# A reciprocal in place of the second decay scan, and four smaller moves, in a gated-linear-attention and router kernel

## The chip, the cores and the metric

The kernel runs on one core of a Trainium2 chip, in one launch. The metric is the device time of that core in microseconds; lower is better.

## What is computed

The first part is gated linear attention over 4 batches, 8 heads, 768 steps and a head size of 48. A state of 48x48 per head decays row by row with alpha and takes in one outer product per step. The second part sends each of the 3072 rows to one of 8 experts, by the largest cosine, and runs that expert's two layers (384 to 1024 to 384).

```python
def _attn_ref(q, k, v, alpha):
    state = np.zeros((B, H, D, D)); y = np.zeros_like(q)
    for t in range(S):
        state = alpha[:, :, t, :, None] * state + np.einsum('bhd,bhe->bhde', k[:, :, t], v[:, :, t])
        y[:, :, t] = np.einsum('bhd,bhde->bhe', q[:, :, t], state)
    return y
...
def _moe_ref(x, expert_emb, tau, w1, w2):
    xn = x / (np.linalg.norm(x, axis=-1, keepdims=True) + 1e-06)
    en = expert_emb / (np.linalg.norm(expert_emb, axis=-1, keepdims=True) + 1e-06)
    logits = xn @ en.T / tau
    expert_idx = np.argmax(logits, axis=1)
    probs = np.exp(logits - logits.max(-1, keepdims=True))
    probs /= probs.sum(-1, keepdims=True) + 1e-09
    gate_w = probs[np.arange(N), expert_idx]
    for e in range(E):
        mask = expert_idx == e
        h = np.maximum(x[mask] @ w1[e], 0.0)
        out[mask] = gate_w[mask, None] * (h @ w2[e])
    return out
```

## The kernel before

**The attention part** works on 24 chunks of 128 steps (6 per batch), all 8 heads at once. The tiles `at`, `kt`, `qt` and `vt` hold alpha, k, q and v of a chunk, with steps on the partitions; heads are padded from 48 to 64 columns. `load` (L410) issues the four transfers of a chunk on SP's queue and clears row 0 of the alpha tile on POOL, after the transfer. `turned` (L400) transposes a tile on PE into PSUM, two heads at a time, which gives four blocks of 128 steps along the free dimension.

`decays` (L420) makes the decay factors within a chunk. Let a(t) be alpha at step t of the chunk. The scan at L433 runs backward over the transposed alpha and leaves in `r` at step t the product of a(t+1) to the chunk's last step; since row 0 of the alpha tile is zero, one scan over all 512 columns restarts at each block. `kr` (L440) is k times `r`. The inverse of `r` is what q needs: a reciprocal of the first column of each block (L443, four elements) is put into the tile `ini`, and a forward scan (L447) multiplies alpha on from there, so that its result `a` is 1/`r` at every step. ACT copies the transposed q out of PSUM (`qc`, L454), and POOL multiplies it by `a` into `qs` (L455). `end` (L450) is the decay over the whole chunk; it takes alpha's first rows from `al0`, a small table of the first row of every chunk, transposed once.

A chunk then goes through a pipeline of several iterations of the main loop (L592): `keys_back` transposes `kr` back (L464) for the state's update, `scores` multiplies `kr` and `qs` (L515) and masks the result on DVE (`sm`, L519), `update` adds to the carried state (L492, L504), `mix_states` and `mix_chunk` make the output (L529, L541), `rows` turns it into rows with logits (L554, L560). `choose` and `place` pick the expert for groups of chunks with short DVE operations and find each token's row; `to_rows` scatters the rows to a buffer `xs` in DRAM through POOL's queue.

Two preparations come after the first chunk's work: `prepare` (L238) loads the expert embeddings, tau and alpha's first rows, normalises the embeddings (`embp`) and fills `sel` and `al0`; `routing_constants` (L111) makes masks and index tables.

**The expert part** starts with an early block of the expert that is first in turn (EARLY = 2 blocks of 128 tokens), whose first layer is already run among the last chunks. `gates` (L684) computes gate weights and output rows: the early block writes them to `gt_s[1]` and `sx_s[1]`, which expert 1 uses as well (L843). `to_rows(pads...)` fills the ends of the experts' blocks in `xs` with blank rows, eight transfers in a row on POOL's queue (L645); `fetch` reads an expert's rows back on SP's queue; `second_layer` ends in `scatter` (L665), an indirect transfer on POOL's queue that reads its row numbers from the `sx` tile.

The order of the work on each engine comes from a scheduler that knows the dependencies and the order of the program text; on each engine, and on each DMA queue, the instructions then run strictly in that order.

Of the kernel before, what the change touches and what calls it, by code (L numbers as in the profile page):

```python
# [27 lines left out]
def kernel(  # L28
# [155 lines left out]
    with ExitStack() as c1:  # L184
# [13 lines left out]
        NR = 3  # L198
        r_s = [keep.tile([P, NP * P], FP32, name=f"r{i}") for i in range(NR)]

        ini_s = [keep.tile([P, NP * P], FP32, name=f"ini{i}") for i in range(2)]
        inr = keep.tile([P, NP * P], FP32, name="inr")

        ND = 3
# [2 lines left out]
        def fixed_parts():  # L207
            for i in range(NBUF):
                nc.gpsimd.memset(at_s[i][:, :, D:DP], 1.0)
                nc.vector.memset(kt_s[i][:, :, D:DP], 0.0)  # L210
                nc.vector.memset(qt_s[i][:, :, D:DP], 0.0)
                if i == 0:
                    nc.gpsimd.memset(inr, 0.0)
                    for p in range(NP - 1):
                        nc.gpsimd.memset(inr[:, p * P + P - 1 : (p + 1) * P], 1.0)
                    for j in range(NR):
                        nc.vector.memset(r_s[j][:, NP * P - 1 :], 1.0)
                if i < 2:
                    nc.vector.memset(ini_s[i], 0.0)
            make_upper_triangular(nc, causal[:, 0], val=1.0, diag=True)  # L220
            for i in range(NBV):
                nc.vector.memset(vt_s[i][:, :, D:DP], 0.0)
            for i in range(ND):
                nc.gpsimd.memset(dec_s[i], 0.0)
# [10 lines left out]

        al0 = keep.tile([P, NP, NS], FP32, name="al0")

        def prepare():  # L238
            emb = work.tile([E, DM], FP32, name="emb", bufs=1)
            nc.scalar.dma_start(out=emb, in_=expert_emb)  # L240
            nc.scalar.dma_start(out=rtau, in_=tau.to_broadcast([P, 1]))
            a0 = work.tile([NS, H, DP], FP32, name="a0", bufs=1)
            nc.gpsimd.memset(a0[:, :, D:DP], 1.0)
            for b in range(B):
                nc.scalar.dma_start(
                    out=a0[b * NCH : (b + 1) * NCH, :, 0:D], in_=a_r[b, :, 0]
                )
            nc.vector.reciprocal(rtau, rtau)
            e2 = work.tile([E, DM], FP32, name="e2", bufs=1)
            en = work.tile([E, 1], FP32, name="en", bufs=1)  # L250
            nc.scalar.activation(e2, emb, AF.Square, accum_out=en)
            nc.scalar.activation(en, en, AF.Sqrt)
            nc.vector.tensor_scalar(en, en, 1e-6, None, ALU.add)
            nc.vector.reciprocal(en, en)
            nc.vector.tensor_tensor(en, en, rtau[:E], ALU.mult)
            embp = work.tile([E, H, DP], FP32, name="embp", bufs=1)
            nc.gpsimd.memset(embp, 0.0)
            nc.vector.tensor_scalar(
                embp[:, :, 0:D], emb.rearrange("e (h d) -> e h d", d=D), en, None, ALU.mult
            )  # L260
            pe = ps_tr.tile([P, NP, E], FP32, tag="tr", name="pe")
            for p in range(NP):
                nc.tensor.transpose(
                    pe[:, p], embp[:, 2 * p : 2 * p + 2].rearrange("e h d -> e (h d)"),
                    ident[:E, :E],
                )
            nc.gpsimd.memset(sel, 0.0)
            for p in range(NP):
                nc.gpsimd.tensor_copy(sel[0:DP, p, 0:D], ident[0:DP, 0:D])
                nc.gpsimd.tensor_copy(sel[DP:P, p, D : 2 * D], ident[DP:P, DP : DP + D])  # L270
            nc.vector.tensor_copy(sel[:, :, 2 * D :], pe)
            p0 = ps_tr.tile([P, NP, NS], FP32, tag="tr", name="p0")
            for p in range(NP):
                nc.tensor.transpose(
                    p0[:, p], a0[:, 2 * p : 2 * p + 2].rearrange("s h d -> s (h d)"),
                    ident[:NS, :NS],
                )
            nc.vector.tensor_copy(al0, p0)

        def to_rows(rows, x):  # L280
            ins = nc.gpsimd.indirect_dma_start(  # L281
# [118 lines left out]
        def turned(t, name):  # L400
# [6 lines left out]
                )  # L407
            return pt

        def load(s):  # L410
            b, c = divmod(s, NCH)
            i = s % NBUF
            nc.sync.dma_start(out=at_s[i][:, :, 0:D], in_=a_r[b, c])

            nc.gpsimd.memset(at_s[i][0:1], 0.0)
            nc.sync.dma_start(out=kt_s[i][:, :, 0:D], in_=k_r[b, c])
            nc.sync.dma_start(out=qt_s[i][:, :, 0:D], in_=q_r[b, c])
            nc.sync.dma_start(out=vt_s[s % NBV][:, :, 0:D], in_=v_r[b, c])

        def decays(s):  # L420

            c = s % NCH
            d = st[s]
            i = s % NBUF
            L = NP * P  # L430
            pa = turned(at_s[i], "pa")
            r = r_s[s % NR]
            nc.vector.tensor_tensor_scan(  # L433
                r[:, L - 2 :: -1], pa[:, L - 1 : 0 : -1], inr[:, L - 2 :: -1],
                1.0, ALU.mult, ALU.add,
            )
            pk = turned(kt_s[i], "pk")
            d["kr"] = kr = work.tile([P, NP, P], FP32, name="kr", bufs=3)
            krf = kr.rearrange("p n t -> p (n t)")
            nc.vector.tensor_tensor(krf, pk, r, ALU.mult)  # L440
            rv = r.rearrange("p (n t) -> p n t", t=P)
            ini = ini_s[s % 2]
            nc.vector.reciprocal(  # L443
                ini.rearrange("p (n t) -> p n t", t=P)[:, :, 0:1], rv[:, :, 0:1]
            )
            a = work.tile([P, L], FP32, name="a")
            nc.vector.tensor_tensor_scan(a, pa, ini, 0.0, ALU.mult, ALU.add)  # L447
            if c > 0:
                d["end"] = end = work.tile([P, NP, 1], FP32, name="end", bufs=3)
                nc.gpsimd.tensor_tensor(end, rv[:, :, 0:1], al0[:, :, s : s + 1], ALU.mult)  # L450
            pq = turned(qt_s[i], "pq")
            d["qs"] = qs = work.tile([P, NP, P], FP32, name="qs", bufs=4)
            qc = work.tile([P, NP * P], FP32, name="qc")
            nc.scalar.copy(qc, pq)  # L454
            nc.gpsimd.tensor_tensor(qs.rearrange("p n t -> p (n t)"), qc, a, ALU.mult)  # L455

        def keys_back(s):

# [129 lines left out]
        send = []  # L588
        fixed_parts()
        load(0)  # L590
        load(1)
        for s in range(NS + 4):  # L592
            if s + 2 < NS:
                load(s + 2)
            if 0 <= s - 1 < NS:
                keys_back(s - 1)
            if 0 <= s - 2 < NS:
                mix_states(s - 2)
            if 0 <= s - 3 < NS:
                rows(s - 3)  # L600
            if s < NS:
                decays(s)
            if 0 <= s - 1 < NS:
                decay_state(s - 1)
                scores(s - 1)
                update(s - 1)
            if 0 <= s - 2 < NS:
                mix_chunk(s - 2)
            if s == 0:
                prepare()  # L610
                routing_constants()
            if 4 <= s < 4 + NXG:
                nc.gpsimd.memset(xg_s[s - 4], 0.0)
            if s == 8:
                nc.gpsimd.memset(blank, 0.0)
            if s == NS:
                turn_early()
                first_layer_early(0, 2)
            if s == NS + 1:
                first_layer_early(2, 4)  # L620

            r = s - 4
            if r >= 0:
                g = group_of[r]
                if r == GROUPS[g][1] - 1:
                    place(g)
                    if r == S0 - 1:
                        first_expert()
            for c in send[:] if s >= S0 + 3 else send[:1]:
                to_rows(dest[:, c : c + 1], st[c]["x"])  # L630
                send.remove(c)
            if r == S0 - 1:
                fetch_early()
                for i in range(2):
                    weights(i)
            r = s - 3
            if 0 <= r < NS:
                g = group_of[r]
                if r == GROUPS[g][1] - 1:
                    choose(g)  # L640
            if s == NS + 2:
                first_layer_early(4, FT)
        counts()
        for i in range(E):
            to_rows(pads[:, i : i + 1], blank)  # L645
            if i < 2:
                fetch(i)


    with ExitStack() as c3:  # L650
# [189 lines left out]
                        half_block(w1_t, w2_t, xT, gate[0:HALF], col[0:HALF])  # L840


        egt, esx = gt_s[1], sx_s[1]  # L843
        gates(exg[:, 0:EARLY], egt[:, 0:EARLY], esx[:, 0:EARLY], EARLY)
        for t in range(EARLY):
            if t == EARLY - 1:
# [7 lines left out]
        for i in range(E):  # L854
            if i + 2 < E:
                weights(i + 2)
                fetch(i + 2)
            run(i)
            run_extra(i)
# [32 lines left out]
```

## Time and profile before

| | us |
|---|---|
| median of 3 runs | 487.36 (486.78 to 490.43) |
| profiled execution, its own time | 490.61 |
| its span, first to last instruction | 488.8 |
| PE busy | 450.3 (92%) |
| DVE busy | 195.1 (40%) |
| POOL busy | 146.8 (30%) |
| ACT busy | 135.3 (28%) |
| mean granted TensorE clock | 0.981 |

The profile is one execution. PE is the matmul engine, PEld its weight loads, DVE the vector engine, ACT the scalar engine, POOL the general engine, SP the engine that issues most of the transfers. A group line reads: source line, engine, operation, output<-inputs by the program's names, shape, count | busy time in us, mean of one in ns | idle time of the engine before them in us, and what ended it. Waits read: engine, tile and line that waited <- what it waited for: us in total, times, the longest. The timeline reads: start in us, length in us, engine, line, operation, count [idle before <- what ended it].

### The profile page before, as it was taken

The numbers are of one execution on the slowest core, as the hardware profiler recorded it, in microseconds if no ns is written. First come the engines' busy times: TensorE is split into PE (matmuls) and PEld (weight loads), VectorE is DVE, ScalarE is ACT, GpSimd is POOL, SyncE is SP. The second block draws the span as 40 slices with busy tenths as digits, with TensorE's granted clock in tenths as the row PEclk, the third lists the DMA queues.
The fourth block names the chain that finished last, engine by engine and source line by source line (L and its number), as shares of the span: only waits on it lengthen the run. The fifth ranks groups of instructions, "written<-read, shape, count | busy, mean of one in ns | idle before, by whom it ended". The sixth has DMA issues, their size and how long they took to land. (4 is left out here: it accounts for less than half of the span.)

```text
span 488.8 us, 8137 instructions
## 1 busy us (share of the span) xinstructions
PE 450.3 (92%) x2964; PEld 327.1 (67%) x2965; DVE 195.1 (40%) x505; ACT 135.3 (28%) x304; POOL 146.8 (30%) x256
## 2 busy tenths in 40 slices
PE   2699979979898999969999999999999999999993
PEld 1699968969787888657555655557556655555551
DVE  3889878887687952530131121110131121111000
ACT  3133323323232323461460240200560160110200
POOL 5855556656545642620101001000101101002001
PEclk9999999999898999988999999999999999999997
DMA  9999877776691297491900903600800710000000
GB/s 142 163 153 163 165 132 165 123 153 134 127 172 25 83 333 268 116 311 56 334 1 34 330 3 106 248 16 19 311 20 34 262 64 32 16 0 34 12 16 31
DMA packets 119189, 59.98 MB, mean 123 GB/s; under 512 B 102119, under 2 KB 113648, under 8 KB 119144
## 3 DMA queue, kind: packets, MB, share of 16 engines
q1 hardware_dynamic: 115040, 49.18, 43.1%
q0 software_dynamic: 3728, 10.16, 5.9%
q8 instruction: 27, 0.44, 0.4%
q14 instruction: 18, 0.15, 0.1%
q10 hardware_dynamic: 376, 0.05, 0.1%
HBM read 49.72 MB, written 11.45 MB: 125 GB/s over the span
## 5 line engine op out<-in xcount | busy, mean ns | idle before, releaser
L728 PE MATMUL ph<-xT,w 128*128 128x384 f32 (+1 forms) x384 | 119.6, 462 | 1.6 <-PEq L813 0.4
L739 PE MATMUL pyo<-w,hT 128*128 128x384 f32 x352 | 118.3, 497 | 0.0
L666 POOL DMA_INDIRECT out_dram<-y,sx x27 | 26.1, 966 | 248.4 <-DVE y L742 171.2
L739 PEld LDWEIGHTS pyo<-w,hT 128*128 128x128 f32 x352 | 67.7, 194 | 46.7 <-issue 2.6
L728 PEld LDWEIGHTS ph<-xT,w 128*128 128x128 f32 x384 | 67.6, 190 | 44.4 <-issue 5.2
L742 DVE TENSOR_SCALAR y<-pyo,gt 128x384 f32<-128x384 f32 x24 | 14.8, 617 | 121.1 <-PE pyo L739 121.1
L732 ACT ACTIVATE hT<-ph 128x384 f32<-128x384 f32 (+1 forms) x64 | 28.5, 459 | 115.6 <-PE ph L728 115.6
L515 PE MATMUL sc<-qs,kr 64*128 64x128 f32 x384 | 30.1, 298 | 12.3 <-POOL qs L455 12.3
L455 POOL TENSOR_TENSOR qs<-qc,a 128x512 f32<-128x512 f32 x24 | 30.5, 1272 | 25.6 <-DVE a L447 22.9
L515 PEld LDWEIGHTS sc<-qs,kr 64*128 64x128 f32 x384 | 25.2, 198 | 16.8 <-POOL qs L455 13.6
L519 DVE TENSOR_TENSOR sm<-sc,causal 128x512 f32<-128x512 f32 x48 | 30.5, 676 | 1.3 <-PE sc L515 1.3
L433 DVE TENSOR_TENSOR_SCAN r<-pa,inr 128x511 f32<-128x511 f32 x24 | 29.2, 1218 | 3.2 <-PE pa L403 2.8
L547 ACT COPY yT<-py 128x512 f32<-128x512 f32 x24 | 14.1, 586 | 58.8 <-PE py L541 58.8
L447 DVE TENSOR_TENSOR_SCAN a<-pa,ini 128x512 f32<-128x512 f32 x24 | 29.3, 1223 | 0.9
L281 POOL DMA_INDIRECT xs<-x,dest x24 | 24.0, 999 | 15.2 <-DVE dest L330 5.2
L541 PE MATMUL py<-sm,vt 128*64 128x128 f32 x384 | 26.5, 282 | 0.0
L682 DVE COPY xT<-pxg 128x384 f32<-128x384 f32 (+1 forms) x30 | 14.7, 498 | 28.9 <-PE pxg L681 28.8
L554 PE MATMUL px<-sel,yT 128*128 128x104 f32 x192 | 25.5, 276 | 0.0
L476 POOL TENSOR_TENSOR dec<-state,end 64x256 f32<-64x256 f32 x40 | 24.3, 608 | 2.7 <-DVE state L504 0.7
L554 PEld LDWEIGHTS px<-sel,yT 128*128 128x128 f32 x192 | 23.4, 192 | 0.8 <-ACT yT L547 0.5
L529 PE MATMUL py<-qs,dec 128*128 128x128 f32 x160 | 22.0, 281 | 0.5 <-DVE state L504 0.5
L541 PEld LDWEIGHTS py<-sm,vt 128*64 128x64 f32 x384 | 21.7, 143 | 0.6
(161 smaller groups left out, 522.5 us busy)
## 6 DMA issues: line engine op xcount, KB each, us to landing
w<-in_moe_w_dram SPq DMA_DIRECT2D x16, 1536.0 KB, 11.4
at<-in_alpha_dram SPq DMA_DIRECT2D x24, 192.0 KB, 5.4
kt<-in_k_dram SPq DMA_DIRECT2D x24, 192.0 KB, 4.0
qt<-in_q_dram SPq DMA_DIRECT2D x24, 192.0 KB, 5.5
vt<-in_v_dram SPq DMA_DIRECT2D x24, 192.0 KB, 3.6
xg<-xs SPq DMA_DIRECT2D x22, 196.5 KB, 6.7
xg<-xs SPq DMA_DIRECT2D x8, 98.2 KB, 5.7
out_dram<-y,sx POOLq DMA_INDIRECT x27, 2.6
```

The source lines that it names most:

```text
L433: nc.vector.tensor_tensor_scan(r[:, L - 2 :: -1], pa[:, L - 1 : 0 : -1], inr[:, L - 2 :: -1], 1.0, ALU.mult, ALU.add,)
L447: nc.vector.tensor_tensor_scan(a, pa, ini, 0.0, ALU.mult, ALU.add)
L455: nc.gpsimd.tensor_tensor(qs.rearrange("p n t -> p (n t)"), qc, a, ALU.mult)
L476: nc.gpsimd.tensor_tensor(dec[sl, :, hh], carried["state"][sl], d["end"][sl].to_broadcast([DP, NP, DP]), ALU.mult,)
L515: nc.tensor.matmul(sc[:, hh, p], lhsT=kr[sl, p], rhs=qs[sl, p], start=True, stop=True)
L519: nc.vector.tensor_tensor(sm[:, hh], sc[:, hh], causal.to_broadcast([P, NP, P]), ALU.mult)
L541: nc.tensor.matmul(py[DP * hh : DP * hh + DP, p], lhsT=vt[:, 2 * p + hh], rhs=sm[:, hh, p], start=("dec" not in d and p == 0), stop=True, ...
L554: nc.tensor.matmul(px[:, p], lhsT=yT[:, p], rhs=sel[:, p], start=True, stop=True)
L666: ins = nc.gpsimd.indirect_dma_start(out=out, out_offset=bass.IndirectOffsetOnAxis(ap=col, axis=0), in_=y, in_offset=None, bounds_check=N - 1,
L728: nc.tensor.matmul(ph, lhsT=w1_t[:, i, f * P : (f + 1) * P], rhs=xT[:, i], start=(i == 0), stop=(i == KT - 1),)
L732: nc.scalar.activation(hT[:, f], ph, AF.Relu)
L739: nc.tensor.matmul(py, lhsT=hT[:, f], rhs=w2_t[:, f], start=(f == 0), stop=(f == FT - 1),)
```

## The change

Six edits. (1) In `decays` the reciprocal is taken of the whole of `r` (128x512, on DVE) and multiplies q; the forward scan, the four-element reciprocal and the `ini` tiles go. (2) Row 0 of the alpha tiles is cleared once at the start; the loads write rows 1 to 127, as two transfers of 112 and 15 rows. (3) The transfer of `vt` of a chunk is issued with the next chunk's loads. (4) The preparations are split: the loads come first, `al0` follows chunk 0's decays, the logits' part chunk 1's, the routing constants chunk 2's; these and the clearing of `xg` and `blank` are queued behind the last DVE and POOL instructions of that chunk's `decays`. (5) Only two of the eight blank fillings stand ahead of the expert part in the text; the other six stand with the fetch of their expert. (6) The early block has gate and row tiles of its own, `egt` and `esx`.

```diff
-        ini_s = [keep.tile([P, NP * P], FP32, name=f"ini{i}") for i in range(2)]
...
         def fixed_parts():
             for i in range(NBUF):
                 nc.gpsimd.memset(at_s[i][:, :, D:DP], 1.0)
+
+                nc.gpsimd.memset(at_s[i][0:1], 0.0)
...
-                if i < 2:
-                    nc.vector.memset(ini_s[i], 0.0)
...
-        def prepare():
-            emb = work.tile([E, DM], FP32, name="emb", bufs=1)
-            nc.scalar.dma_start(out=emb, in_=expert_emb)
-            nc.scalar.dma_start(out=rtau, in_=tau.to_broadcast([P, 1]))
+        emb = work.tile([E, DM], FP32, name="emb", bufs=1)
+
+        def prepare_loads():
             a0 = work.tile([NS, H, DP], FP32, name="a0", bufs=1)
-            nc.gpsimd.memset(a0[:, :, D:DP], 1.0)
+            nc.vector.memset(a0[:, :, D:DP], 1.0)
             for b in range(B):
                 nc.scalar.dma_start(
                     out=a0[b * NCH : (b + 1) * NCH, :, 0:D], in_=a_r[b, :, 0]
                 )
+            nc.scalar.dma_start(out=emb, in_=expert_emb)
+            nc.scalar.dma_start(out=rtau, in_=tau.to_broadcast([P, 1]))
+            return a0
+
+        def prepare_first(a0):
+
+            p0 = ps_tr.tile([P, NP, NS], FP32, tag="tr", name="p0")
+            for p in range(NP):
+                nc.tensor.transpose(
+                    p0[:, p], a0[:, 2 * p : 2 * p + 2].rearrange("s h d -> s (h d)"),
+                    ident[:NS, :NS],
+                )
+            nc.vector.tensor_copy(al0, p0)
+
+        def prepare_logits():
+
             nc.vector.reciprocal(rtau, rtau)
...
+        AROW = P - 15
+
         def load(s):
...
+            if s < NS:
+                b, c = divmod(s, NCH)
+                i = s % NBUF
+                for p0, p1 in ((1, AROW), (AROW, P)):
+                    nc.sync.dma_start(out=at_s[i][p0:p1, :, 0:D], in_=a_r[b, c, p0:p1])
+                nc.sync.dma_start(out=kt_s[i][:, :, 0:D], in_=k_r[b, c])
+                nc.sync.dma_start(out=qt_s[i][:, :, 0:D], in_=q_r[b, c])
+            if s > 0:
+                b, c = divmod(s - 1, NCH)
+                nc.sync.dma_start(out=vt_s[(s - 1) % NBV][:, :, 0:D], in_=v_r[b, c])
+
+        def behind(s):
+
+            queue = ExitStack()
+            for call in st[s]["last"]:
+                queue.enter_context(tc.issue_after(call.ins))
+            return queue
 
         def decays(s):
...
             pk = turned(kt_s[i], "pk")
+            ri = work.tile([P, L], FP32, name="ri")
+            nc.vector.reciprocal(ri, r)
             d["kr"] = kr = work.tile([P, NP, P], FP32, name="kr", bufs=3)
             krf = kr.rearrange("p n t -> p (n t)")
-            nc.vector.tensor_tensor(krf, pk, r, ALU.mult)
-            rv = r.rearrange("p (n t) -> p n t", t=P)
-            ini = ini_s[s % 2]
-            nc.vector.reciprocal(
-                ini.rearrange("p (n t) -> p n t", t=P)[:, :, 0:1], rv[:, :, 0:1]
-            )
-            a = work.tile([P, L], FP32, name="a")
-            nc.vector.tensor_tensor_scan(a, pa, ini, 0.0, ALU.mult, ALU.add)
-            if c > 0:
-                d["end"] = end = work.tile([P, NP, 1], FP32, name="end", bufs=3)
-                nc.gpsimd.tensor_tensor(end, rv[:, :, 0:1], al0[:, :, s : s + 1], ALU.mult)
+            by_dve = nc.vector.tensor_tensor(krf, pk, r, ALU.mult)
...
-            nc.gpsimd.tensor_tensor(qs.rearrange("p n t -> p (n t)"), qc, a, ALU.mult)
+            by_pool = nc.gpsimd.tensor_tensor(
+                qs.rearrange("p n t -> p (n t)"), qc, ri, ALU.mult
+            )
+            if c > 0:
+                d["end"] = end = work.tile([P, NP, 1], FP32, name="end", bufs=3)
+                rv = r.rearrange("p (n t) -> p n t", t=P)
+                nc.gpsimd.tensor_tensor(end, rv[:, :, 0:1], al0[:, :, s : s + 1], ALU.mult)
+            d["last"] = by_dve, by_pool
...
         load(0)
+        a0 = prepare_loads()
         load(1)
         for s in range(NS + 4):
-            if s + 2 < NS:
+            if s + 2 <= NS:
                 load(s + 2)
...
+            if s == 0:
+                with behind(s):
+                    prepare_first(a0)
...
-            if s == 0:
-                prepare()
-                routing_constants()
+            if s == 1:
+                with behind(s):
+                    prepare_logits()
+            if s == 2:
+                with behind(s):
+                    routing_constants()
             if 4 <= s < 4 + NXG:
-                nc.gpsimd.memset(xg_s[s - 4], 0.0)
+                with behind(s):
+                    nc.gpsimd.memset(xg_s[s - 4], 0.0)
             if s == 8:
-                nc.gpsimd.memset(blank, 0.0)
+                with behind(s):
+                    nc.gpsimd.memset(blank, 0.0)
...
-        for i in range(E):
+        for i in range(2):
             to_rows(pads[:, i : i + 1], blank)
-            if i < 2:
-                fetch(i)
+            fetch(i)
...
-        egt, esx = gt_s[1], sx_s[1]
+        egt = xp.tile([P, EARLY], FP32, name="egt")
+        esx = xp.tile([P, EARLY], I32, name="esx")
...
             if i + 2 < E:
                 weights(i + 2)
+                to_rows(pads[:, i + 2 : i + 3], blank)
                 fetch(i + 2)
             run(i)
```

More of the change, by code (lines that the diff above doesn't have):

```diff
@@ L271, in prepare @@
             nc.vector.tensor_copy(sel[:, :, 2 * D :], pe)
[L272 to L276, printed above, removed]
-                )
-            nc.vector.tensor_copy(al0, p0)
         def to_rows(rows, x):
@@ L408, in turned @@
             return pt
+        AROW = P - 15
         def load(s):
[L411 to L418, printed above, removed]
+            if s < NS:
[13 more added lines that the diff above has]
+            return queue
         def decays(s):
@@ L437, in decays @@
             pk = turned(kt_s[i], "pk")
+            ri = work.tile([P, L], FP32, name="ri")
+            nc.vector.reciprocal(ri, r)
             d["kr"] = kr = work.tile([P, NP, P], FP32, name="kr", bufs=3)
             krf = kr.rearrange("p n t -> p (n t)")
-            nc.vector.tensor_tensor(krf, pk, r, ALU.mult)
-            rv = r.rearrange("p (n t) -> p n t", t=P)
-            ini = ini_s[s % 2]
-            nc.vector.reciprocal(
-                ini.rearrange("p (n t) -> p n t", t=P)[:, :, 0:1], rv[:, :, 0:1]
-            )
-            a = work.tile([P, L], FP32, name="a")
-            nc.vector.tensor_tensor_scan(a, pa, ini, 0.0, ALU.mult, ALU.add)
-            if c > 0:
-                d["end"] = end = work.tile([P, NP, 1], FP32, name="end", bufs=3)
-                nc.gpsimd.tensor_tensor(end, rv[:, :, 0:1], al0[:, :, s : s + 1], ALU.mult)
+            by_dve = nc.vector.tensor_tensor(krf, pk, r, ALU.mult)
             pq = turned(qt_s[i], "pq")
```

## The prediction

> **What bounds the kernel now.** I read the busy tenths first, to see which engine fills which stage.
>
> ```profile
> PE   2699979979898999969999999999999999999993
> DVE  3889878887687952530131121110131121111000
> ```
>
> A slice is 12.2 us. Up to slice 14 (about 170 us) the 24 attention chunks run, with PE and DVE both at 7 to 9 tenths; from there on PE is at 9 and DVE nearly idle. The expert stage belongs to PE, and nothing in the change shortens PE's work. So the attention stage decides, and in it the two busiest engines. The windows give their shares and a clock that I need later:
>
> ```profile
> 24.00:170.00 146.00, 134.18 (x1630) 122.93 (x1629) 122.17 (x248) 46.81 (x102) 85.28 (x151) 0.98 0.73 132
> 217.20:224.00 6.80, 6.09 (x12) 3.56 (x13) 2.34 (x10) 1.62 (x6) 0.00 (x0) 0.50 0.70 254
> ```
>
> Columns: window, length, busy PE, PEld, DVE, ACT, POOL, PE clock, DMA share, GB/s. From 24 to 170 us PE is busy 92%, DVE 84%, POOL 58%. The timeline has the first scan (L433) of chunk 2 at 24.5 and of chunk 23 at 170.0 us: 21 chunks in 145.5 us, 6.93 us each, of which DVE works 122.17 / 21 = 5.82. The best six chunks (24.5 to 60.9) take 6.07 each. PE sets the pace, with about 1.1 us of slack on DVE per chunk. The groups show the operations in question and the one stall of PE:
>
> ```profile
> L515 PE MATMUL sc<-qs,kr 64*128 64x128 f32 x384 | 30.1, 298 | 12.3 <-POOL qs L455 12.3
> L433 DVE TENSOR_TENSOR_SCAN r<-pa,inr 128x511 f32<-128x511 f32 x24 | 29.2, 1218 | 3.2 <-PE pa L403 2.8
> L447 DVE TENSOR_TENSOR_SCAN a<-pa,ini 128x512 f32<-128x512 f32 x24 | 29.3, 1223 | 0.9
> ```
>
> PE waits 12.3 us in all for qs, six times: where choose puts its small operations ahead on DVE.
>
> **The reciprocal.** Removed per chunk: the scan L447, 1.22 us, and the four-element reciprocal L443, whose ordinary duration is 0.17 (its mean of 0.22 holds one of 1.43). Added: a reciprocal of 128x512. No row shows one that large. The nearest are the small ones of the gates, beside another operation at the same place:
>
> ```profile
> L711 DVE RECIPROCAL gt<-gt 128x4 f32<-128x4 f32 x7 | 1.2, 178 | 0.2
> L710 DVE TENSOR_SCALAR gt<-gt 128x4 f32<-128x4 f32 x7 | 1.2, 169 | 0.2
> L710 DVE TENSOR_SCALAR gt<-gt 128x2 f32<-128x2 f32 x2 | 0.3, 168 | 0.1
> L711 DVE RECIPROCAL gt<-gt 128x2 f32<-128x2 f32 x2 | 0.3, 166 | 0.1
> ```
>
> Two more elements cost the reciprocal 12 ns and TENSOR_SCALAR 1 ns. A reduction goes from 170 ns (128x16, L709) to 183 (128x32), under 1 ns an element. So the reciprocal's slope is 6 ns an element: 178 + 508 x 6 = 3226 ns. The cheap end takes kr (L440, 128x512 in 718 ns) as one pass at the ordinary rate: 0.7 us. The dear end puts all that the four-element row has above a one-element operation on its elements: above L255 (147 ns) that is 31 / 4 = 7.8 ns and 4.1 us for 512, above L253 (142 ns) 9 ns and 4.7 us. I take 3.2, the difference between rows of the same operation at the same place; 0.7 and 4.1 to 4.7 stay for the range.
>
> The Trainium skill ("VectorE: DVE Perf Modes", section "Walkthrough: the 8-slice pipeline in each mode") says that Reciprocal runs on an iterative divide with a repeat count of 8, which speaks against this edit. Read as 8 cycles an element, at the 0.96 GHz that the skill gives VectorE ("Trainium Kernel Development and Optimization", section "NeuronCore Architecture"), that would be an estimated 4.3 us and a total near 532 us; the measured 12 ns for two elements fits it only in part.
>
> DVE per chunk becomes 5.82 - 1.22 - 0.17 + 3.23 = 7.66 us, more than PE's 6.07. The bound changes hands. An engine that bounds is still not busy all the time (DVE's best ten microseconds, 165 to 175, show 9.62), and pa of the next chunk stands on PE behind pkb, which waits for kr, and kr now stands behind the reciprocal. At 95% a chunk is 8.05 us: 21 x 8.05 = 169.1, against 145.5: **+23.6**.
>
> **The beginning.** The timeline from 4 to 12 us:
>
> ```profile
> 4.77 1.11 PE L403 MATMUL pa<-ident,at 128*128 128x128 f32 x4 [4.77 <-POOL at L415]
> 9.92 0.51 POOL L415 MEMSET at<- 1x512 f32 x1 [5.21 <-DMA at<-in_alpha_dram]
> 10.53 0.51 POOL L257 MEMSET embp<- 8x512 f32 x1
> 11.08 0.56 DVE L258 TENSOR_SCALAR embp<-emb,en 8x384 f32<-8x384 f32 x1 [2.80 <-POOL embp L257]
> 11.57 1.20 DVE L433 TENSOR_TENSOR_SCAN r<-pa,inr 128x511 f32<-128x511 f32 x1
> ```
>
> pa of chunk 0 is on PE at 4.8, its scan on DVE only at 11.6: DVE stands at embp, which waits for POOL, where the memset of row 0 waits for the second alpha load. The change takes both away (row 0 is cleared once, ahead of all loads; embp comes after chunk 1). The scan then starts at about 5.9. Chunk 1 follows after 1.22 + 3.23 + 0.70 and cold pkb and pa of 1.1 each, 7.3 us later (13.2), chunk 2 some 7.7 later (20.9, against 24.5): **-3.6**. What was moved now lies on the engine that bounds: the logits' six DVE operations (1.3 us) and the routing constants (L119 to L122, 3.4 us here, two of them stretched beyond 1 us beside a memset on POOL). I count **+2** of at most 4.7. The moved POOL work (sel, embp, three xg memsets of 1.40, blank 0.42) goes behind qs on POOL, which has 42% free; without that cover it is some 8 us.
>
> **The loads.** 24 memsets of 0.516 go, 12.4 us of POOL that cost nothing after the start. 24 more DMAs are issued on SP, at 0.37 to about 0.5 us; SP mostly waits for buffers, so only the first counts, and it is offset by the half microsecond of memset before pa. vt one chunk later and its buffer long free: nothing; the data of a chunk took SP some 4.9 us at the start, less than a chunk.
>
> **The end.** After the last scan the reciprocal ends 3.2 us later where the old pair, with kr, took 2.1: **+1.1**, partly covered by the early expert's matmuls. Then the own egt and esx. Around 215 us the waits are:
>
> ```profile
> DVE sx L700 <- DMA out_dram<-y,sx: 5.2, 1, 5.2
> PE pxg L681 <- DVE xT L682: 3.7, 1, 3.7
> ```
>
> sx of expert 1 may not be written until the early scatter has read its indices; the xT copies stand behind it on DVE, and PE stops for 3.7 us. Then comes the window at clock 0.50 above: the 16 matmuls pyo take 8.2 us there, where 26 took 8.63 at full clock (5.3 for 16), 2.9 more. With own tiles both go: at most 6.6, at least nothing if the rows of expert 1 are what is late next. I take **-5**. The skill's "TensorE: Matmul & The Clock Gate" (Part 1, the HAM clock gate) lets half rate follow an idle window of about 3.4 us, which fits this stop; by its rule the 2.9 goes with the stop. Six of eight pads still stand ahead of the first scatter; two fewer save 2.6 us of POOL, which PE does not wait for.
>
> **Sum.** 23.6 - 3.6 + 2 + 1.1 - 5 = +18.1 us. The profiled execution took 490.6 (span 488.8); the median of the runs is 487.4, so I put 18 on that: 505.
>
> **Rivals.** (1) The reciprocal is cheap, 0.7 us: DVE falls to 5.1 us a chunk, PE stays the bound, the stalls for qs shrink. 21 chunks at about 6.3 are 132 (-13), the beginning gains 7 (chunk 2's scan at about 16, since its alpha had landed by the memset at 15.7, less the moved small operations), the end 5: 462, 25 us faster. For it: reductions and TENSOR_TENSOR run at 1 ns an element, and 12 ns on so small an operation is near the scatter of those rows (one reciprocal of four took 166). Against it: 13 of 14 four-element ones lie at 177 or 178. The sign turns where the reciprocal takes about 2.4 us (a chunk of 7.2), 4.4 ns an element. (2) The dear end: at 4.1 us a chunk is busy 8.53 and takes 8.98, +43 for 21 chunks and +40 with the other terms (chunk 2's scan at 22.7, the tail at +2.0): 528; at 4.7 likewise 543; in the middle 535. (3) About 2.3 us and an even result, 488, if part of the 12 ns is a fixed cost. That the reciprocal were not executed or merged away is not possible: it is one instruction per chunk on DVE ahead of kr.
>
> **Chances.** Forecast (492 to 516, reciprocal 2.7 to 3.6 us) 0.55; dear 0.20; cheap 0.19; even 0.06. A measurement tells about 1% from no change here. Faster comes from the cheap case, slower from the first two and little of the third: 0.19, 0.05, 0.76. The range leaves out the cheap case and reaches to the dear end: 485 to 536; the forecast's own is 492 to 516.
>
> **What would show it.** The 128x512 reciprocal near 3.2 us; DVE above 93% from 20 to 190 us and PE nearer 75%, waiting for kr at pkb instead of for qs; first scan at 6 us, last near 190; no wait for the scatter before expert 1. It is wrong if the reciprocal's row shows under 2.4 us, or if PE's waits for kr grow so long that the clock column falls to 0.5 in the chunks.

## The result, and the profile after

| | before | after |
|---|---|---|
| median, us | 487.37 (486.78 to 490.43) | 514.18 (511.8 to 518.37) |
| profiled execution, span, us | 488.8 | 516.6 |
| mean granted TensorE clock | 0.981 | 0.952 |

The change makes the kernel slower: the ratio is 1.0546 (95% interval 1.046 to 1.0632). The busy tenths of the page, in 40 slices of 12.9 us:

```profile
PE   4899587897779878999999999999999999999994
DVE  5799878899798988233212111110121021111000
```

The attention chunks now reach into slice 16 (the last scan starts at 197.7 us), and within them PE has mostly 7 and 8 where it had mostly 9. The groups that answer to those shown before (line, engine, operation, output<-input, shape, count | busy us, mean ns | idle before, and what ended it):

```profile
L459 DVE RECIPROCAL ri<-r 128x512 f32<-128x512 f32 x24 | 80.4, 3352 | 0.4
L453 DVE TENSOR_TENSOR_SCAN r<-pa,inr 128x511 f32<-128x511 f32 x24 | 29.2, 1216 | 14.6 <-PE pa L410 14.4
L534 PE MATMUL sc<-qs,kr 64*128 64x128 f32 x384 | 31.6, 303 | 5.8 <-POOL qs L467 3.0
```

The reciprocal is the costliest operation on DVE, 80.4 us where the scan had 29.3. The wait of PE for qs fell from 12.3 to 3.0 us. What PE waits for instead, by total, times and longest:

```profile
PE rk L325 <- POOL before L316: 12.5, 4, 3.7
PE pkb L483 <- DVE kr L462: 8.9, 6, 4.6
PE py L548 <- POOL dec L495: 5.2, 3, 1.9
```

pkb waits for kr, which stands behind the reciprocal, as forecast; rk is new: the matmuls of `place` wait for the counts (`before`, on POOL) that follow the expert choice, whose small DVE operations stand around the reciprocal. The window from the third scan to the last (columns as before: length, busy PE, PEld, DVE, ACT, POOL, clock, DMA share, GB/s):

```profile
22.75:197.68 174.93, 145.13 (x1612) 131.87 (x1611) 157.28 (x228) 46.20 (x102) 82.24 (x147) 0.91 0.61 111
```

DVE is busy 90% of it and PE 83%; before they were at 84% and 92%. The mean hides two kinds of chunk. In sixteen of the 21, from scan to scan, DVE is busy 97%, and they take 7.76 us on average (one of them 9.9, with 9.2 of DVE's work). The other five take 9.3 to 11.0 us and hold 13.5 of the 17.7 us in which DVE stands idle. In each of the five, or just ahead of it, PE stops for 1.9 to 4.6 us, and the granted clock is 0.72 to 0.85. One chunk of each kind:

```profile
22.75:31.27 8.52, 8.52 (x80) 7.53 (x80) 8.39 (x16) 1.89 (x4) 4.01 (x15) 0.78 1.11 153
128.48:138.93 10.45, 7.13 (x76) 6.60 (x75) 7.36 (x12) 1.97 (x4) 3.28 (x8) 0.84 0.42 77
```

The two spans, cut at three events that the timeline of both shows:

| stretch, us | before | after | difference | forecast |
|---|---|---|---|---|
| start to the scan of chunk 2 | 24.47 | 22.75 | -1.7 | -3.6, +2 |
| to the scan of chunk 23 (21 chunks) | 145.5 | 174.9 | +29.4 | +23.6 |
| to the early expert's second layer | 25.8 | 32.1 | +6.3 | +1.1 |
| to the end | 293.0 | 286.9 | -6.2 | -5 |
| sum | 488.8 | 516.6 | +27.8 | +18.1 |

### The profile page after: what moved, and what is told of

The parts are those of the page before. It is cut to its first block, busy times and chain, and to the rows that moved or that the text cites. A ratio compares the mean times of both kernels' runs of the same rounds, so it can differ in the third digit from the quotient of the medians.

```text
span 516.6 us, 8083 instructions
## 1 busy us (share of the span) xinstructions
PE 466.1 (90%) x2964; PEld 340.7 (66%) x2965; DVE 233.3 (45%) x480; ACT 135.2 (26%) x304; POOL 137.6 (27%) x235
## 5 line engine op out<-in xcount | busy, mean ns | idle before, releaser
L766 PE MATMUL pyo<-w,hT 128*128 128x384 f32 x352 | 115.6, 488 | 0.0
L766 PEld LDWEIGHTS pyo<-w,hT 128*128 128x128 f32 x352 | 66.3, 190 | 45.3
L693 POOL DMA_INDIRECT out_dram<-y,sx x25 | 24.1, 965 | 239.1 <-DVE y L769 168.9
L459 DVE RECIPROCAL ri<-r 128x512 f32<-128x512 f32 x24 | 80.4, 3352 | 0.4
L467 POOL TENSOR_TENSOR qs<-qc,ri 128x512 f32<-128x512 f32 x24 | 30.5, 1271 | 58.3 <-DVE ri L459 29.4
L534 PE MATMUL sc<-qs,kr 64*128 64x128 f32 x384 | 31.6, 303 | 5.8 <-POOL qs L467 3.0
L453 DVE TENSOR_TENSOR_SCAN r<-pa,inr 128x511 f32<-128x511 f32 x24 | 29.2, 1216 | 14.6 <-PE pa L410 14.4
L548 PE MATMUL py<-qs,dec 128*128 128x128 f32 x160 | 27.8, 322 | 7.0 <-POOL dec L495 5.2
L548 PEld LDWEIGHTS py<-qs,dec 128*128 128x128 f32 x160 | 23.9, 226 | 9.7 <-POOL dec L495 5.9
L573 PE MATMUL px<-sel,yT 128*128 128x104 f32 x192 | 28.5, 293 | 1.5 <-ACT yT L566 1.5
L573 PEld LDWEIGHTS px<-sel,yT 128*128 128x128 f32 x192 | 26.2, 210 | 2.4 <-ACT yT L566 2.1
```

The lines of the kernel that those rows point to most:

```text
L453: nc.vector.tensor_tensor_scan(r[:, L - 2 :: -1], pa[:, L - 1 : 0 : -1], inr[:, L - 2 :: -1], 1.0, ALU.mult, ALU.add,)
L459: nc.vector.reciprocal(ri, r)
L467: by_pool = nc.gpsimd.tensor_tensor(qs.rearrange("p n t -> p (n t)"), qc, ri, ALU.mult)
L534: nc.tensor.matmul(sc[:, hh, p], lhsT=kr[sl, p], rhs=qs[sl, p], start=True, stop=True)
L548: nc.tensor.matmul(py[:, p], lhsT=dec[:, p].rearrange("p j e -> p (j e)"), rhs=d["qs"][:, p], start=(p == 0), stop=False, skip_group_check ...
L573: nc.tensor.matmul(px[:, p], lhsT=yT[:, p], rhs=sel[:, p], start=True, stop=True)
```

## The experiments

Theory A is that of the prediction: the reciprocal makes DVE the bound of the chunks, and the other edits gain at the start and behind the early expert. Theory B: the moved preparations and the order of the work cost the time. Theory C: not DVE's work, but the chain from the scan through reciprocal, kr and the transposes on PE to the next scan sets the chunk.

### One edit, or all but one

The first edit alone, on the kernel of before:

```diff
...
+            a = work.tile([P, L], FP32, name="ri")
+            nc.vector.reciprocal(a, r)
             nc.vector.tensor_tensor(krf, pk, r, ALU.mult)
             rv = r.rearrange("p (n t) -> p n t", t=P)
-            ini = ini_s[s % 2]
-            nc.vector.reciprocal(
-                ini.rearrange("p (n t) -> p n t", t=P)[:, :, 0:1], rv[:, :, 0:1]
-            )
-            a = work.tile([P, L], FP32, name="a")
-            nc.vector.tensor_tensor_scan(a, pa, ini, 0.0, ALU.mult, ALU.add)
```

> Only the first edit on the kernel of before: the 128x512 reciprocal in place of the second scan, everything else as it was. Theory A (the reciprocal makes DVE the bound of the chunks): the chunks cost about 29 us more as in the changed kernel (174.9 against 145.5 us from the third scan to the last), the first two chunks some 3 us more, the way from the last scan to the early expert's second layer some 6 us more, and nothing is given back at the start and the end: about 525 us (515 to 532), above the changed kernel. Theory B (the moved preparations and the new order of the work cost the time, the reciprocal is not the main thing): below 500 us.

Measured: 530.93 us, ratio 1.0873 (1.0804 to 1.0942), above the changed kernel and at the upper end of A's range. Chunks 179.4 us, last scan to second layer 32.0, third scan at 27.8. B falls as the main cause.

The other five edits, with the scan kept:

```diff
-            ri = work.tile([P, L], FP32, name="ri")
-            nc.vector.reciprocal(ri, r)
...
+            ini = ini_s[s % 2]
+            nc.vector.reciprocal(
+                ini.rearrange("p (n t) -> p n t", t=P)[:, :, 0:1], rv[:, :, 0:1]
+            )
+            a = work.tile([P, L], FP32, name="a")
+            by_dve = nc.vector.tensor_tensor_scan(a, pa, ini, 0.0, ALU.mult, ALU.add)
...
```

> The changed kernel with the second scan and the four-element reciprocal put back in place of the 128x512 reciprocal; the other five edits stay. Theory A: the third scan comes at 17 to 19 us instead of 24.5, the chunks take about 6.9 us each as before, the end gains 6 us: about 475 us (470 to 480). Theory B (the moves cost time): 487 us or more.

Measured: 480.42 us, ratio 0.9828 (0.9761 to 0.9895), at the upper edge of A's 470 to 480. The third scan comes at 19.6 (expected 17 to 19), the 21 chunks take 145.9 (before 145.5), the end is 5.5 us shorter. So the moves gain 8 to 10 us in all and leave the chunks' pace alone. Some of the start is given back there: from the second scan to the third it takes 8.9 us, against 5.4 before. The moved work lies between these chunks; in the changed kernel PE stops there for 2.2 us until POOL is past the first moved filling (embp).

The sixth edit alone:

```diff
-        egt, esx = gt_s[1], sx_s[1]
+        egt = xp.tile([P, EARLY], FP32, name="egt")
+        esx = xp.tile([P, EARLY], I32, name="esx")
```

> Only the sixth edit on the kernel of before: own gate and row tiles of the early block. If the 6.2 us that the changed kernel gains behind the early expert come from the wait for the scatter (3.7 us of PE, and 2.9 us at half clock behind it): 481 us (479.5 to 483). If they come from the fewer blank fillings ahead of the first scatter: 487 us, no change.

Measured: 482.09 us against 488.72 beside it, ratio 0.988 (0.9847 to 0.9913). From the second layer of the early expert to the end it takes 286.5 us, as after the whole change (286.9), against 293.0 before. The stop of PE at pxg is not among its waits any more, and no window at half clock follows (clock 1.00 from 204 to 224 us). The gain of the end is this edit's, and not that of the fewer blank fillings. Its longest waits of PE, which are those of before without the 3.7 us for xT:

```profile
PE sc L515 <- POOL qs L455: 11.3, 6, 3.2
PE pe L263 <- DVE kr L440: 7.3, 1, 7.3
PE pa L403 <- POOL at L415: 4.8, 1, 4.8
PE py L529 <- DVE state L504: 0.5, 1, 0.5
```

### DVE's work, or the chain through PE

kr ahead of the reciprocal on DVE:

```diff
-            ri = work.tile([P, L], FP32, name="ri")
-            nc.vector.reciprocal(ri, r)
...
-            by_dve = nc.vector.tensor_tensor(krf, pk, r, ALU.mult)
+            kr_ins = nc.vector.tensor_tensor(krf, pk, r, ALU.mult)
+            ri = work.tile([P, L], FP32, name="ri")
+            with tc.issue_after(kr_ins.ins):
+                by_dve = nc.vector.reciprocal(ri, r)
```

> The changed kernel with kr ahead of the reciprocal on DVE, so that the transposes of kr on PE no longer wait behind the reciprocal. Theory A (DVE's own work sets the chunk): only DVE's idle time ahead of the scan can go, 14.4 us in all, of which a part comes back as other waits: 502 to 513 us. Theory C (the chain scan, reciprocal, kr, transposes on PE, next scan sets the chunk, not DVE's work): below 497 us. If q's side was already as late as k's: 514 us or more.

Measured: 512.79 us, ratio 1.0474 (1.0398 to 1.0551), at the upper end of A's range and far from C's. The chunks take 174.7 us, the same as after the change (174.9), although DVE's idle time ahead of the scan fell from 14.6 to 5.0 us:

```profile
L453 DVE TENSOR_TENSOR_SCAN r<-pa,inr 128x511 f32<-128x511 f32 x24 | 29.1, 1212 | 5.0 <-PE pa L410 4.9
```

What DVE waits for in the chunks instead:

```profile
DVE state L524 <- POOL dec L496: 8.7, 3, 3.4
DVE lg L580 <- PE px L574: 6.1, 6, 2.1
DVE r L453 <- PE pa L410: 2.2, 4, 1.6
```

The wait moved. PE's wait for kr at pkb fell from 8.9 to 0.9 us, and its wait for qs rose from 3.0 to 14.0:

```profile
PE sc L535 <- POOL qs L468: 14.0, 4, 4.0
```

In the chunks this is the third case of what was expected: q's side was as late as k's. That the later qs is also what makes the state's update late on POOL is argued and not shown. C, with its chain through kr, falls as the one cause. The few us by which the whole is shorter lie behind the last scan (26.1 instead of 32.1 us), at the place of the half clock told of below.

### How the chunk follows the reciprocal's length

```diff
...
-            ri = work.tile([P, L], FP32, name="ri")
-            nc.vector.reciprocal(ri, r)
+            ri = ri_s[s % 2]
+            nc.vector.reciprocal(ri[:, 0 : L // 2], r[:, 0 : L // 2])
```

and likewise with L // 4.

> The changed kernel with the reciprocal taken of the first 256 of 512 columns; the other half of ri keeps the value 1, so q of the heads there is not divided by the decay. The reciprocal's own row first: 178 + 252 x 6.25 = 1753 ns, if its cost is a fixed part and 6.25 ns an element. Threshold theory (DVE bounds while its work per chunk is above PE's): DVE per chunk is (157.28 - 70.39) / 21 + 1.75 = 5.9 us, under PE's 6.07; the chunks fall back to PE's pace, 6.6 to 6.9 us each, and the whole to about 480 us (475 to 484), near the kernel with the moves only (480.4). Linear theory (every microsecond of reciprocal lies on the path): 514 - 24 x 1.6 = 476 us, not to be told apart here, only together with the quarter.

> The same with the first 128 columns only, the rest of ri keeps the value 1. The reciprocal takes 178 + 124 x 6.25 = 953 ns. Threshold theory: PE is already the bound with the half, so the quarter gives no more than the stalls for qs that shrink: within 6 us of the half (473 to 482). Linear theory: 19 us below the half, about 457 us. This is also about what the change would have brought if the reciprocal had been as cheap as an ordinary operation (rival 1, 462 us).

Measured: 490.66 and 473.27 us (ratios 1.0045, 1.0008 to 1.0082, and 0.9686, 0.9645 to 0.9728). Another q sends tokens to other experts, so the expert part is not the same work (3028 matmuls in the whole run, 2964 after the change): from the early second layer to the end it takes 295.5 and 296.0 us instead of 286.9. With 286.9 in its place the spans would be 480.2 and 463.8. The stretches before that can be compared. The rows of the reciprocal, from each of the two:

```profile
L462 DVE RECIPROCAL ri<-r 128x256 f32<-128x256 f32 x24 | 42.1, 1752 | 0.9
```

```profile
L462 DVE RECIPROCAL ri<-r 128x128 f32<-128x128 f32 x24 | 22.8, 952 | 0.9
```

952, 1752 and 3352 ns lie on one line, 152 + 6.25 n; it gives 177 ns for four elements, where most small rows of the gates had 177 and 178. The windows from the third scan to the last, of the quarter and of the half:

```profile
17.86:151.85 133.99, 129.65 (x1616) 118.87 (x1615) 114.86 (x231) 46.19 (x103) 82.68 (x148) 1.00 0.84 150
```

```profile
18.84:167.86 149.02, 134.58 (x1620) 122.53 (x1620) 130.22 (x232) 46.53 (x101) 83.09 (x148) 0.98 0.77 134
```

Divided by 21 chunks, with the window of the changed kernel from above:

| reciprocal of | 128 | 256 | 512 columns |
|---|---|---|---|
| its time, us | 0.95 | 1.75 | 3.35 |
| DVE busy per chunk, us | 5.47 | 6.20 | 7.49 |
| PE busy per chunk, us (clock) | 6.17 (1.00) | 6.41 (0.98) | 6.91 (0.91) |
| chunk, us | 6.38 | 7.10 | 8.33 |

The chunk of the half is outside what was expected of it (6.6 to 6.9), and DVE's work with it is 6.20 us and not 5.9. Neither theory of the two expectations holds as it was put. The linear one asked for 0.80 between quarter and half and 1.60 between half and whole, and 0.72 and 1.23 were measured. The threshold one had quarter and half within 6 us of each other, and 15 us of chunks lie between them. With the quarter PE is busy 97% and sets the pace. With the half neither engine fills the chunk (PE 90%, DVE 87%), and it is at least 0.7 us longer than the busy time of either. Here too the loss lies in single chunks: 9.7 of the 15 us between quarter and half are in four chunks that take 8.8 to 10.0 us with the half.

### The wait for the choice

```diff
+            late = s - 5
+            if 0 <= late < S0 - 3 and late == GROUPS[group_of[late]][1] - 1:
+                place(group_of[late])
             r = s - 4
             if r >= 0:
                 g = group_of[r]
                 if r == GROUPS[g][1] - 1:
-                    place(g)
+                    if r >= S0 - 3:
+                        place(g)
```

> The changed kernel with place of the first five groups one iteration later, so that its matmuls on PE (rk) no longer wait for the expert choice that stands on DVE behind the reciprocal. Those waits are 12.5 us in all, and a window at half clock follows most of them. If the chunks that run 8.3 to 11 us instead of 7.4 are long because PE stops there: the chunks fall from 174.9 to 158 to 165 us, the whole to 498 to 506. If DVE's work alone sets the chunks: 511 to 517, no change. The way from the last scan may differ by 6 us by where a half-clock window falls.

Measured: 510.72 us, ratio 1.045 (1.0404 to 1.0495); chunks 169.5 us. A miss: the time lies between the two cases that were expected, close to that of no change. The wait of rk fell from 12.5 to 5.0 us and the chunks gave 5.4, while other waits grew:

```profile
PE pkb L483 <- DVE kr L462: 8.3, 10, 2.6
PE py L548 <- POOL dec L495: 8.1, 2, 4.4
PE sc L534 <- POOL qs L467: 5.4, 3, 2.7
PE rk L325 <- POOL before L316: 5.0, 2, 2.6
```

Eighteen of the 21 chunks now take 7.6 us on average, with DVE busy 98%. Three take 9.9 to 11.8 us, at a clock of 0.71 to 0.83, and hold 11.7 of the 14.0 us in which DVE stands idle. So the long chunks became fewer and not shorter. What makes them long is not settled by this run.

### More work for PE

The score matmuls twice, in the changed kernel and in that of before:

```diff
-            for p in range(NP):
+            for p in [*range(NP)] * 2:
                 for hh in range(2):
                     sl = slice(DP * hh, DP * hh + DP)
                     nc.tensor.matmul(
                         sc[:, hh, p], lhsT=kr[sl, p], rhs=qs[sl, p], start=True, stop=True
...
```

> The changed kernel with the score matmuls (8 per chunk) run twice into the same place; the result is the same. It adds about 1.1 us of PE per chunk at full clock, 26 us in all. If DVE is the bound of the chunks: most of it falls into PE's idle time (29.8 us of the chunks' 174.9), and the whole goes up by 0 to 10 us (514 to 524). If PE is still the bound, by its waits and its half clock: 20 us or more (534 or more).

> The kernel of before with the score matmuls run twice, the control to the same edit on the changed kernel (which moved 514.18 to 514.66 us). If PE is the bound of the chunks before the change: 1.1 us more per chunk, 26 us in all, less at most the 12.3 us that PE stood waiting for qs: 501 to 514 us. If DVE already was the bound before: under 495 us.

Measured: on the changed kernel 514.66 us, ratio to before 1.053 (1.0478 to 1.0582), no change against 1.0546: the chunks take 2.0 us more, the stretch behind the last scan 3.7 less. On the kernel of before 501.0 against 490.52 beside it, ratio 1.02 (1.0155 to 1.0244), with the wait for qs down from 12.3 to 2.4 us. The windows over the chunks, of the kernel of before with doubled scores and of the changed one with them:

```profile
24.00:175.00 151.00, 148.23 (x1951) 137.36 (x1951) 123.57 (x247) 46.45 (x101) 84.67 (x149) 1.00 0.70 127
```

```profile
22.36:199.23 176.87, 155.00 (x1950) 143.00 (x1949) 163.02 (x231) 46.46 (x101) 84.14 (x148) 0.97 0.60 115
```

The doubled matmuls, of the kernel of before (30.1 us without doubling):

```profile
L515 PE MATMUL sc<-qs,kr 64*128 64x128 f32 x768 | 50.6, 281 | 2.4 <-POOL qs L455 2.4
```

So they add 0.85 us a chunk and not the 1.1 of the expectation; on the changed kernel it is 0.81 (51.0 for 31.6 us in all). In the first window PE is busy 98%: it is the bound, and the added work shows (chunks 145.5 to 152.0; most of the rest took the place of the wait for qs). In the second the chunks go from 174.9 to 176.9 us, although PE is busy 9.9 us longer. DVE is busy 92% there, and what PE waits for is now kr, in 19 places, while the wait of rk has gone:

```profile
PE pkb L483 <- DVE kr L462: 21.4, 19, 2.7
```

This shows the change of the bound, with one limit: the clock is higher too (0.97 for 0.91), which may hide a part of the added work. One chunk can be compared directly, that from the third scan to the fourth. It took 8.52 us at a clock of 0.78 after the change (above), and here it takes the same at 1.00, with DVE busy 8.39 us in both:

```profile
22.36:30.88 8.52, 7.39 (x92) 6.66 (x90) 8.39 (x15) 1.91 (x4) 5.00 (x16) 1.00 1.23 160
```

Where DVE filled the chunk, PE's low clock cost nothing. In the five long chunks of the changed kernel the low clock comes together with stops of PE, and no run separates the two.

### The moves with place later

The edits of the moves alone and of place later, together.

> The kernel with the five other edits and the second scan kept (480.4 us), and place of the first five groups one iteration later. Its PE waits 12.3 us for qs, in the chunks of 8.6 to 10.6 us after each choice, where DVE's small operations and three scatters on POOL stand ahead of the second scan and of qs. If place's matmuls and scatters, falling into the same chunk as the choice, are what makes those chunks long: 473 to 477 us. If the choice's own operations are: 479 to 482 us.

Measured: 476.74 us against 490.52 beside it, ratio 0.9711 (0.9682 to 0.9741); chunks 142.4 us, the wait for qs 4.9 instead of 12.3 us. It keeps the second scan and beats both kernels. The shift of place gave the chunks 3.5 us here (145.9 without it) and 5.4 beside the reciprocal, so it is not shown to be worth more with the one bound than with the other.

## Why the prediction was right, point by point

**The bound before, and the change of it.** Right: doubled PE work lengthens the chunks by 6.5 us before and by 2.0 after. The chance of 0.76 for slower was on the right case; 514.2 lies in the forecast's own range (492 to 516), near its upper end. That range was drawn for the length of the reciprocal, which was nearly as forecast. What used it up were two other terms, 5.8 us in the chunks and 5.2 behind the last scan, so that the total still lies inside is partly luck. Of the signs that were named, the reciprocal's row, the early first scan and the missing wait for the scatter came. DVE at 89% and PE at 83% from 20 to 194 us (93% and 75% named), the last scan at 197.7 (190) and rk as PE's largest wait did not.

**The reciprocal's length.** 3.35 us against 3.23. The step from two rows of 12 ns apart gave 6 ns an element; it is 6.25. That the small rows already lay on the line could not be seen from them, since DVE rows of that size scatter by some 12 ns: the 24 four-element reciprocals of L443 took 170 ns in the median and 164 at the least, and against 166 for two elements they would have given 2 ns an element or less. The prediction left them out of its count of 13 in 14. The slope was right by a choice of rows that the record did not force, which is luck in part. The rule of the Trainium skill ("VectorE: DVE Perf Modes", section "Walkthrough: the 8-slice pipeline in each mode") pointed the right way, to an iterative divide; its repeat count of 8, read as 8 cycles an element, gave an estimated 4.3 us, and the measurement decides: 6.25 ns is 6 cycles at the 0.96 GHz of "Trainium Kernel Development and Optimization" (section "NeuronCore Architecture").

**The chunks.** The term was mis-sized: 23.6 forecast, 29.4 measured. The step "at 95% a chunk is 8.05 us" spread the loss over all chunks, and it is not spread. DVE's work per chunk was even below the forecast (7.49 instead of 7.66), and in sixteen chunks DVE was busy 97%, at 7.76 us a chunk. The miss lies in the five of 9.3 to 11.0 us, each with a stop of PE at rk, pkb or py and a clock of 0.72 to 0.85. Whether the stop or the clock behind it makes them long was not separated. Taking away most of the wait at rk gave 5.4 us, taking away that at pkb nothing.

**The beginning.** First scan at 5.2 (5.9 forecast), second at 12.5 (13.2), third at 22.7 (20.9, and +2 for the moved operations): the sum was right, in part by luck: the two microseconds come between chunk 1 and chunk 2 (10.2 us; 7.7 and part of the 2 forecast), where PE stops 2.2 us for embp on POOL and DVE then waits for PE; they are not the busy time of DVE where I had put them.

**From the last scan to the second layer.** Forecast +1.1, measured +6.3: the other mis-sized term. The window of the changed kernel:

```profile
203.90:214.10 10.20, 10.03 (x53) 8.52 (x54) 4.13 (x14) 0.80 (x3) 3.94 (x8) 0.50 1.03 390
```

PE is busy all of it, at half clock; if PE sets the pace there, that is some 5 us lost. The first edit alone has such a window there as well (10.2 us at 0.5, 32.0 us for the stretch); kr first, the moves alone and the quarter have none and take 26.1, 25.8 and 25.0. It is not the whole of it everywhere: with place later 6.8 us at half clock stand in a stretch of 31.0. That the window follows PE's waits in the last chunks (1.9 us for the choice just ahead of it) is argued from the order of events and was not tried by itself. The prediction had named a clock of 0.5 in the chunks as a sign of being wrong, without a price and not for this stretch. In the chunks it did come in places (0.50 from 184 to 190 us), with 0.91 as the mean.

**The end.** Forecast -5, measured -6.2, and -6.6 for the edit alone: the stop of 3.7 us and the half clock behind it, 6.6 together, went entirely. The rule of "TensorE: Matmul & The Clock Gate" (Part 1) on an idle window of some 3.4 us agrees: without the stop the window at 0.50 is not there. It does not fit the half clock behind the last scan, where the waits of PE just ahead are only 0.2 and 1.9 us; there the measurement decides.

**The rivals.** With a reciprocal of 0.95 us the span would be 463.8, near the 462 of the first rival. The turn was put at 2.4 us: with the third scan at 19.5, 25.8 from the last scan on and 286.9 for the rest, 156.6 us of chunks make 488.8; on a straight line between the half (149.0) and the whole (174.9) that is an estimated 2.2 us.

## What to carry to other kernels

A count of DVE operations says nothing of their length: measure a small and a larger form of an operation before it takes the place of two cheaper ones, and compare its time with the slack of the engine in that stage, here 1.1 us a chunk against 1.96 us added. When an engine becomes the bound, do not spread one share of idle time over all stretches: here DVE was busy 97% in most chunks, and the loss lay in five where PE had stopped. Look for those stops, and price the clock of PE where PE takes over again. Edits that are bundled should be run one by one: five of these six gain 8 to 10 us together, and the first hid it.

## What the runs showed of the hardware

A reciprocal of fp32 on DVE takes 152 ns and 6.25 ns for each element of a partition (952, 1752 and 3352 ns for 128, 256 and 512), which makes 3352 ns for 128x512 where the multiplication of the same size took 647 to 718. Half clock on PE is not a loss in itself: the same chunk took 8.52 us at a clock of 0.78 and of 1.00 where DVE was busy 8.39 of it, while the stretch behind the last scan took 32 us with 10 us at half clock in it and 25 to 27 without, where no work was added.
